# Where the first loads of float64 weights stand in a linear-attention and mixture-of-experts kernel, and where the later ones are asked for

## The chip, the cores and the metric

The kernel runs on one core of one Trainium2 chip. The metric is device microseconds (us) of one execution, the median of several runs. One profiled execution gives the rows below. PE is the matrix engine (TensorE), DVE the vector engine, ACT the scalar engine, POOL is GpSimd, and SP is the queue (SyncE) that issues the DMA transfers. Lxxx is a line of the kernel's source.

## The reference, cut to what matters

```python
def phi(x):                                   # attention feature map, 64 -> 256
    proj = einsum('bhsd,df->bhsf', x, w_phi)
    proj = proj - max(abs(proj), axis=-1)
    return concatenate([exp(proj), exp(-proj)])
q_p, k_p = phi(q), phi(k)                     # 4 batches, 8 heads, 576 rows, 64 wide
kv  = einsum('bhsf,bhsd->bhfd', k_p, v);  z = k_p.sum(axis=2)
x   = einsum('bhsf,bhfd->bhsd', q_p, kv) / (einsum('bhsf,bhf->bhs', q_p, z) + 1e-6)
x   = x as (2304, 512)
h   = x @ w_in;  x = maximum(0.01 * h, h) @ w_out     # 512 x 2048, 2048 x 512, float64
p   = probs / (probs.sum(-1) + 1e-9)                  # 2304 x 4
out = sum over 4 experts of p[:, e] * (maximum(x @ w1[e], 0) @ w2[e])
```

`w_in` and `w_out` arrive as float64, and the kernel takes them apart into float32 itself.

## The kernel before, in words

The work is four batches of attention, each followed by the first feed-forward layer on its 576 tokens, and then the four experts on all tokens. Every float32 matrix is split into a high part and a rest (`hilo`, L113), and a product is three matmuls of the parts.

**Attention.** A batch has four pairs of heads. For each pair the steps of the list STEPS run: loads of k, q and v (`kraw`, `qraw`, `v`), the projections on PE (`pq` for q, `pk` for k), the subtraction of the maximum (`mb`, `ky`), exponentials (`e`, `kp`, `kt`), the state `kvp` and `kv`, the numerator `nm` and its copy `nf`, and the division: a row of `nf` goes through DMA into `ds` (L352), is inverted on DVE (L359, L360), stored to DRAM as `dr` (L362), read back over 64 partitions as `rb` (L365), and multiplied into `xr` (L381), which is split into `xh` and `xl`.

**First feed-forward layer.** 16 tiles of 128 hidden columns for each batch: `up` (L506) makes `hp` from `xh`/`xl` and a tile of `w_in`; `hs`, `g` and `gt` are the leaky relu and its split; `down` (L538) makes `op` from four `gt` and four tiles of `w_out`. Groups of four tiles, in the order of the list ORDER.

**Float64 weights.** For the first batch `w64_dma` loads two 128 x 512 float64 tiles (1 MB) as `r64` (shown as `r` by the profile) into a pool of ten buffers. `w64_split` decodes a tile: ACT takes the high words (L460), DVE shifts and joins sign and low words (L461, L464, L467), the float32 tile `w32` is stored to DRAM (L471) for the later batches, and `hilo` splits it into `wt`. `w1_dma` and `w1_split` ask for a load and a decoding by number of tile: `w1_dma(0, F)` is `w_in`, `w1_dma(1, F)` is `w_out`, and in the first batch only even F load, two tiles at once. Later batches load `w32` back.

**Order.** The steps are sorted by hand-set times and written out in that order: `first()` loads the first weights at a set time within the attention of batch 0, `first2()` decodes the first tile, and `up(F, n)`, n = 0 and 1 for the two halves of a tile, asks for the next loads and decodings. A scheduler then simulates the engines and decides in which order each engine and the SP queue take the instructions. Those under `tc.keep_in_program_order` keep their order among themselves. Every queue and engine works in order: what waits holds up all that is behind it.

In `first()` of before, the tile loaded by `w1_dma(1, 0)` is loaded again by `up(0, 0)`, and only the second copy is read.

Of the kernel before, what the change touches and what calls it, by code (L numbers as in the profile page):

```python
# [9 lines left out]
U32 = mybir.dt.uint32  # L10
# [10 lines left out]
NF = FF1 // 128  # L21
# [58 lines left out]
def body(ctx, tc, kT, qT, vh, w_phi, w_in, w_out, probs, w1, w2, out):  # L80
    nc = tc.nc
# [336 lines left out]
    def attn(b, lo, hi):  # L418

        A = []  # L420
        for p in range(NP):
            T = TIMES[p if b == 0 else NP]
            for t, (f, h, a) in zip(T, STEPS):
                i = p if h is None else 2 * p + h
                A.append((p + t, lambda f=f, i=i, a=a: f(b, i, *a)))
        A.sort(key=lambda x: x[0])
        t0, t1 = A[0][0], A[-1][0]
        return [(lo + (hi - lo) * (t - t0) / (t1 - t0), f) for t, f in A]
# [4 lines left out]
    def w_dma(key, src):  # L433
        raw[key] = wrp.tile([128, 512], F32, tag="wr", name="wr")
        nc.sync.dma_start(out=raw[key], in_=src)

    def w_split(key, b, r=None):
        t = wp.tile([128, 2, 512], F32R, tag="w", name="wt")
        hilo(t[:, 0], t[:, 1], raw.pop(key) if r is None else r, 'w', b)
        return t  # L440

    def w64_dma(i, f):

        t = xp.tile([128, 2, 512, 2], U32, tag="x", name="r64")
        nc.sync.dma_start(
            out=t.rearrange("p a c t -> p a (c t)"),
            in_=(w_in, w_out)[i][f : f + 2].bitcast(U32).rearrange("a p c -> p a c"),
        )
        raw[i, f] = t[:, 0]
        raw[i, f + 1] = t[:, 1]  # L450

    def w64_split(i, f):

        r = raw.pop((i, f))
        lo, hi = r[:, :, 0], r[:, :, 1]
        w = wrp.tile([128, 512], F32, tag="wr", name="w32")
        wu = w.bitcast(U32)


        nc.scalar.activation(out=w, in_=hi.bitcast(F32), func=AF.Abs, scale=2.0**-112)  # L460
        nc.vector.tensor_scalar(  # L461
            out=wu, in0=wu, scalar1=3, scalar2=None, op0=ALU.logical_shift_left
        )
        nc.vector.scalar_tensor_tensor(  # L464
            out=wu, in0=hi, scalar=0x80000000, in1=wu, op0=ALU.bitwise_and, op1=ALU.bitwise_or
        )
        nc.vector.scalar_tensor_tensor(  # L467
            out=wu, in0=lo, scalar=29, in1=wu, op0=ALU.logical_shift_right, op1=ALU.bitwise_or
        )
        d = drw.tile([128, 512], F32, name=f"w32_{i}_{f}")  # L470
        nc.sync.dma_start(out=d, in_=w)  # L471
        w32[i, f] = d
        return w_split(None, 1, w)
# [4 lines left out]
    def w1_dma(i, F):  # L478
        b, f = divmod(F, NF)
        if b == 0:  # L480
            if f % 2 == 0:
                w64_dma(i, f)
        elif b < B:
            w_dma((i, F), w32[i, f])

    def w1_split(i, F):
        b, f = divmod(F, NF)
        if b < B:
            wt1[i, F] = w64_split(i, f) if b == 0 else w_split((i, F), b + 1)
# [7 lines left out]
    def moe1_up(F, n):  # L497
        x = xs[F // NF]
        wi = wt1[0, F]
        if n == 0:  # L500
            hps[F] = two("hp")
        hp = hps[F]
        for kk in range(KK):
            assert ("x", F // NF, kk) in made
            for i, (a, z) in enumerate(PASS):
                nc.tensor.matmul(  # L506
                    hp[:, n, 0:HS],
                    lhsT=wi[:, a, kk * 128 : (kk + 1) * 128],
                    rhs=x[z][:, kk, n * HS : (n + 1) * HS],
                    start=(kk == 0 and i == 0),  # L510
                    stop=(kk == KK - 1 and i == 2),
                )
        if n == 0:
            return
        hv = hp[:, :, 0:HS]
        hs = unit("hs")
        hs3 = hs.rearrange("p (a s) -> p a s", a=2)
        nc.scalar.mul(out=hs3, in_=hv, mul=0.01)
        g = unit("g")
        nc.vector.tensor_tensor(  # L520
            out=g.rearrange("p (a s) -> p a s", a=2), in0=hv, in1=hs3, op=ALU.max
        )
        gt = gp.tile([128, 2, S], F32R, tag="g", name="gt")
        hilo(gt[:, 0], gt[:, 1], g, 'g', F // NF + 1)
        gts[F] = gt
# [3 lines left out]
    def moe1_down(C, d, n):  # L529
        b, c = divmod(C, NF // GF)  # L530
        if c == 0 and d == 0 and n == 0:
            accs[b] = xp.tile([128, KK, S], F32, tag="x", name="acc")
        if n == 0:
            ops[C, d] = two("op")
        op = ops[C, d]
        for f in range(GF):
            for i, (a, z) in enumerate(PASS):
                nc.tensor.matmul(  # L538
                    op[:, n, 0:HS],
                    lhsT=wt1[1, C * GF + f][:, a, d * 128 : (d + 1) * 128],  # L540
                    rhs=gts[C * GF + f][:, z, n * HS : (n + 1) * HS],
                    start=(f == 0 and i == 0),
                    stop=(f == GF - 1 and i == 2),
                )
        if n == 0:
            return
        av = accs[b][:, d].rearrange("p (a s) -> p a s", a=2)
        if c == 0:
            nc.scalar.copy(out=av, in_=op[:, :, 0:HS])
        else:  # L550
            nc.vector.tensor_tensor(out=av, in0=op[:, :, 0:HS], in1=av, op=ALU.add)  # L551

    def moe1_group(G):


        def up(F, n):
            if n == 0:
                w1_dma(0, F + 2)
                w1_split(0, F + 1)
                w1_dma(1, F)  # L560
            elif F:
                w1_split(1, F - 1)
            moe1_up(F, n)

        def down(d, n):
            if G == B * NF // GF and d == 0 and n == 0:
                w1_split(1, G * GF - 1)
            moe1_down(G - 1, d, n)

        M = []  # L570
        for kind, i in ORDER:
            if kind == "u" and G < B * NF // GF:
                M += [lambda i=i, n=n: up(G * GF + i, n) for n in range(2)]
            elif kind == "d" and G > 0:
                M += [lambda i=i, n=n: down(i, n) for n in range(2)]
        return M
# [139 lines left out]
    def product(k, i, out, first):  # L716
        a, b = PRODUCTS[i]
        ws, xo = wo[k], xops[k // NC2][b]
        n = 0
        for kk in range(2):  # L720
            for w, z in PASS:
                kept(nc.tensor.matmul(  # L722
                    out,
                    lhsT=ws[w][:, AOPS[a], kk * 128 : (kk + 1) * 128],
                    rhs=xo[z][:, kk],
                    start=first and n == 0,
                    stop=n == 5,
                    skip_group_check=not first,
                ))
                n += 1  # L730
# [111 lines left out]
    def spread(fs, lo, hi):  # L842
        return [(lo + (hi - lo) * i / len(fs), f) for i, f in enumerate(fs)]

    def first():
        w1_dma(0, 0)
        w1_dma(1, 0)

    def first2():
        w1_split(0, 0)  # L850

    plan = attn(0, -P0, 0) + [(-P0 * (1 - FI0), first), (-P0 * (1 - FI1), first2)]
    for b in range(B):
        m = []
        for G in range(b * NF // GF, (b + 1) * NF // GF):
            m += spread(moe1_group(G), G * GF / NF, (G + 1) * GF / NF)
        if b + 1 < B:
            a = attn(b + 1, b + LO[b], b + HI[b])
        else:
            early = x2_steps(0)  # L860
            a = spread(early[:4], b + 0.1, b + 0.9)
# [27 lines left out]
    n = NB * NC2  # L889
# [3 lines left out]
    for k in range(n):  # L893
        j, c = divmod(k, NC2)
# [43 lines left out]
```

## Time and profile before

| | |
|---|---|
| median of 3 runs | 1379.69 us (1378.5 to 1380.32) |
| the profiled execution's own time | 1380.63 us |
| its span in the trace | 1378.8 us |
| mean granted clock of PE | 0.992 |
| busy: PE | 1352.1 us, 98% |
| busy: DVE | 817.8 us, 59% |
| busy: ACT | 657.9 us, 48% |
| busy: POOL | 567.8 us, 41% |
| loads of `w_in` / `w_out`, 1 MB each | 8 / 9 |

The span is the time from the first to the last instruction in the trace. The difference of 1.8 us to the execution's time lies around it. PE is idle for 26.7 us in all, most of it in the first 110 us, where attention and feed-forward layer of batch 0 and the decoding of weights share DVE and ACT.

### The profile page before, as it was taken

To read this page: it belongs to the slowest core of one execution; us is meant where nothing else is said; L and a number is where in the kernel's file an instruction comes from. 1 tells how busy PE (TensorE), PEld (TensorE's weight loads), DVE (VectorE), ACT (ScalarE), POOL (GpSimd) and SP (SyncE) were. 2 spreads that over 40 slices of the span, in tenths; PEclk is the share of its full clock that TensorE was granted. 3 is DMA by queue.
4 is the path that set the end of the run, shared out by engine and by line. 5 is a ranking of instruction groups with operands and counts; after the bars stand their busy time and mean duration, and the time that the engine had idled before them with its cause. 6 is when DMAs were issued, how large, how long until landed. Compare 5 with 4: busy or idle time off the path is not lost.

```text
span 1378.8 us, 21301 instructions
## 1 busy us (share of the span) xinstructions
PE 1352.1 (98%) x8105; PEld 1262.2 (92%) x8105; DVE 817.8 (59%) x1285; ACT 657.9 (48%) x1201; POOL 567.8 (41%) x398
## 2 busy tenths in 40 slices
PE   8979999999999999999999999999999999999998
PEld 6778999999999999998999999999999999899997
DVE  4589999678786656553555445445454444554444
ACT  5657657676576435424343443434443343433331
POOL 3211102111111000027767666767767675565651
PEclk9989999999999999999999999999999999999999
DMA  6466645333332222302212122321121232122111
GB/s 220 113 217 234 220 167 166 111 120 105 109 103 66 75 86 73 104 24 94 75 61 77 62 68 71 107 77 62 62 77 62 77 107 77 62 64 76 61 62 62
DMA packets 78518, 134.94 MB, mean 98 GB/s; under 512 B 12240, under 2 KB 22608, under 8 KB 78416
## 3 DMA queue, kind: packets, MB, share of 16 engines
q1 hardware_dynamic: 78416, 133.58, 29.8%
q8 instruction: 64, 1.05, 0.3%
q14 instruction: 38, 0.31, 0.1%
HBM read 120.30 MB, written 13.18 MB: 97 GB/s over the span
## 4 chain that ended last, share of the span: by engine, by line
PE 95%; DVE 1%; DMA 1%; issue 1%; ACT 1%; POOL 1%; SPq 0%; POOLq 0%; ACTq 0%; DVEq 0%
PE po L761 29%; PE hp L506 15%; PE op L538 14%; PE py L722 11%; PE pv L722 7%; PE px L722 7%; PE kvp L242 5%; PE nm L335 4%; PE pk L204 2%; PE pq L292 1%; PE pq L289 1%; DMA qraw<-qT 1%; POOL wul L704 0%; DMA r<-w 0%; DMA ds<-nf 0%
## 5 line engine op out<-in xcount | busy, mean ns | idle before, releaser
L761 PE MATMUL po<-wd,gh 128*128 128x512 f32 x1152 | 387.7, 391 | 0.9 <-POOL wd L714 0.9
L777 DVE SCALAR_TENSOR_TENSOR ob<-po,pe,ob 128x512 f32<-128x512 f32 x270 | 201.6, 749 | 216.6 <-PE po L761 216.6
L761 PEld LDWEIGHTS po<-wd,gh 128*128 128x128 f32 x1152 | 216.6, 188 | 42.3 <-POOL wd L714 1.3
L761 PE MATMUL po<-wd,gl 128*128 128x512 f32 x576 | 226.2, 393 | 0.0
L538 PE MATMUL op<-gt,wt 128*128 128x288 f32 x1536 | 219.9, 297 | 1.5 <-DVE gt L118 0.8
L296 POOL PARTITION_ALL_REDUCE mb<-pc x32 | 72.3, 2266 | 355.7 <-ACT pc L294 294.7
L506 PE MATMUL hp<-xh,wt 128*128 128x288 f32 x1024 | 216.2, 298 | 0.0
L538 PEld LDWEIGHTS op<-gt,wt 128*128 128x128 f32 x1536 | 207.9, 188 | 2.9 <-DVE gt L118 1.0
L506 PEld LDWEIGHTS hp<-xh,wt 128*128 128x128 f32 x1024 | 167.5, 188 | 1.0 <-ACT wt L117 0.3
L506 PE MATMUL hp<-xl,wt 128*128 128x288 f32 x512 | 151.8, 297 | 0.0
L714 POOL TENSOR_TENSOR wd<-r,wd 128x1024 fp32r<-128x1024 f32 x48 | 114.9, 2394 | 89.4 <-ACT wd L710 89.4
L722 PE MATMUL py<-xo,wuh 128*128 128x384 f32 x576 | 148.3, 339 | 0.7 <-DVE pz L827 0.7
L682 POOL TENSOR_TENSOR rs<-r 128x256 f32<-128x256 f32 x96 | 71.1, 741 | 188.8 <-DMA r<-w 188.8
L704 POOL TENSOR_TENSOR wul<-rs,wuh 128x1024 fp32r<-128x1024 f32 x48 | 115.5, 2406 | 65.9 <-ACT wuh L699 65.9
L704 POOL TENSOR_TENSOR wul<-r,wuh 128x768 fp32r<-128x768 f32 x48 | 88.8, 1851 | 85.7 <-ACT wuh L699 85.7
L761 PEld LDWEIGHTS po<-wd,gl 128*128 128x128 f32 x576 | 108.2, 188 | 15.2
L722 PEld LDWEIGHTS py<-xo,wuh 128*128 128x128 f32 x576 | 104.9, 188 | 4.6 <-DVE pz L827 1.0
L722 PE MATMUL px<-xo,wuh 128*128 128x384 f32 x384 | 98.9, 338 | 0.7 <-DVE acc L551 0.7
L722 PE MATMUL pv<-xo,wuh 128*128 128x384 f32 x384 | 99.1, 339 | 0.0
L722 PE MATMUL py<-xo,wul 128*128 128x384 f32 x288 | 97.3, 338 | 0.0
L506 PEld LDWEIGHTS hp<-xl,wt 128*128 128x128 f32 x512 | 96.3, 188 | 0.4
L807 ACT COPY py<-px 128x384 f32<-128x384 f32 x48 | 22.2, 463 | 143.4 <-PE px L722 137.3
(114 smaller groups left out, 2349.9 us busy)
## 6 DMA issues: line engine op xcount, KB each, us to landing
r<-w SPq DMA_DIRECT2D x192, 256.0 KB, 2.8
wr<-w SPq DMA_DIRECT2D x96, 256.0 KB, 2.7
qraw<-qT SPq DMA_DIRECT2D x32, 288.0 KB, 3.7
r<-w_out SPq DMA_DIRECT2D x9, 1024.0 KB, 9.0
r<-w_in SPq DMA_DIRECT2D x8, 1024.0 KB, 6.2
w<-w SPq DMA_DIRECT2D x32, 256.0 KB, 2.8
v<-vh SPq DMA_DIRECT2D x16, 480.0 KB, 4.0
kraw<-kT SPq DMA_DIRECT2D x16, 288.0 KB, 4.0
```

The source lines that it names most:

```text
L204: nc.tensor.matmul(o, lhsT=x[:, cs], rhs=w, start=(i == 0), stop=(i == len(P) - 1))
L242: nc.tensor.matmul(kvp[:, a * 128 : (a + 1) * 128], lhsT=lhs, rhs=v[:, c, h * D : h * D + 128], start=(c == 0), stop=(c == 4),)
L296: nc.gpsimd.partition_all_reduce(mb, pc, 128, bass_isa.ReduceOp.absmax)
L335: nc.tensor.matmul(o, lhsT=a[:, 2 * (h % 2) + j], rhs=x[:, j * HS : (j + 1) * HS], start=(j == 0 and i == 0), stop=(j == 1 and i == len(P) ...
L506: nc.tensor.matmul(hp[:, n, 0:HS], lhsT=wi[:, a, kk * 128 : (kk + 1) * 128], rhs=x[z][:, kk, n * HS : (n + 1) * HS], start=(kk == 0 and i ...
L538: nc.tensor.matmul(op[:, n, 0:HS], lhsT=wt1[1, C * GF + f][:, a, d * 128 : (d + 1) * 128], rhs=gts[C * GF + f][:, z, n * HS : (n + 1) * HS ...
L682: kept(nc.gpsimd.tensor_tensor(out=o, in0=x, in1=y, op=op))
L704: kept(nc.gpsimd.tensor_tensor(out=lo[:, at], in0=(r[:, 1:4], s)[i], in1=hi[:, at].bitcast(F32), op=ALU.subtract))
L714: kept(nc.gpsimd.tensor_tensor(out=d[:, 1], in0=r2, in1=d[:, 0].bitcast(F32), op=ALU.subtract))
L722: kept(nc.tensor.matmul(out, lhsT=ws[w][:, AOPS[a], kk * 128 : (kk + 1) * 128], rhs=xo[z][:, kk], start=first and n == 0, stop=n == 5, ski ...
L761: kept(nc.tensor.matmul(op, lhsT=(gh, gl)[z][:, 2 * f + t, q : q + 128], rhs=d[:, w, f], start=n == 0, stop=n == 5,))
L777: kept(nc.vector.scalar_tensor_tensor(out=o, in0=op, scalar=ps, in1=o, op0=ALU.mult, op1=ALU.add))
```

## The change

`first()` asks for the tiles 0/1 and 2/3 of `w_in`, and no longer for `w_out`. `up` leaves out the load of `w_in` for F = 0, and asks for `w_out` at n = 1 in the first batch (half a tile after `w_in`), at n = 0 later. The first batch then makes 8 loads of each. All float64 loads are kept in program order behind what was kept before them.

```diff
@@ w64_dma
-        nc.sync.dma_start(
-            out=t.rearrange("p a c t -> p a (c t)"),
-            in_=(w_in, w_out)[i][f : f + 2].bitcast(U32).rearrange("a p c -> p a c"),
+        tc.keep_in_program_order(
+            nc.sync.dma_start(
+                out=t.rearrange("p a c t -> p a (c t)"),
+                in_=(w_in, w_out)[i][f : f + 2].bitcast(U32).rearrange("a p c -> p a c"),
+            )
         )
@@ moe1_group
         def up(F, n):
             if n == 0:
-                w1_dma(0, F + 2)
+                if F:
+                    w1_dma(0, F + 2)
                 w1_split(0, F + 1)
+            if n == (F < NF):
                 w1_dma(1, F)
-            elif F:
+            if n and F:
                 w1_split(1, F - 1)
             moe1_up(F, n)
@@ body
     def first():
         w1_dma(0, 0)
-        w1_dma(1, 0)
+        w1_dma(0, 2)
```

The change adds lines, so the lines behind it are 2 to 5 higher: the loads stand at L447, the decoding at L463, L464, L467 and L470, the stores at L474, `up` at L509 and `down` at L541.

**First place: the SP queue at 9 to 25 us.** `qraw_182` is the last q load issued at 9.29 us, and `v_184` the v load of head pair 2, which shares a buffer with `v_125` of pair 0. Before:

```order
L166 DMA qraw_182<-qT 128x576
L445 DMA r64_207<-w_in 128x2x1024
L445 DMA r64_209<-w_out 128x2x1024
L161 DMA v_184<-vh 128x5x192
L166 DMA qraw_226<-qT 128x576
L471 DMA w32_0_0_476<-w32_471 128x512
```

And now:

```order
L166 DMA qraw_182<-qT 128x576
L161 DMA v_184<-vh 128x5x192
L447 DMA r64_207<-w_in 128x2x1024
L447 DMA r64_209<-w_in 128x2x1024
L166 DMA qraw_226<-qT 128x576
L474 DMA w32_0_0_476<-w32_471 128x512
```

Both float64 loads moved behind `v_184`, and the second is now of `w_in`.

**Second place: ACT, and PE, at 25 to 36 us.** `w32_471` and the next `w32` are the decoding of the first two tiles of `w_in`, `pc` is the eviction of a `pq`, `kp` and `kt` are exponentials of k. ACT before:

```order
L460 ACTIVATE w32_471<-r64_207 128x512
L460 ACTIVATE w32_621<-r64_207 128x512
L227 ACTIVATE kt_170<-pk_214 128x256 x2
L342 COPY nf_221<-nm_222 128x288
L342 COPY nf_228<-nm_229 128x288
L294 COPY pc_244<-pq_241 128x576
L117 CAST wt_478<-w32_471 128x512
L342 COPY nf_228<-nm_233 128x288
L294 COPY pc_251<-pq_248 128x576
L342 COPY nf_221<-nm_237 128x288
```

And now:

```order
L227 ACTIVATE kt_170<-pk_214 128x256 x2
L342 COPY nf_221<-nm_222 128x288
L342 COPY nf_228<-nm_229 128x288
L294 COPY pc_244<-pq_241 128x576
L463 ACTIVATE w32_471<-r64_207 128x512
L463 ACTIVATE w32_619<-r64_207 128x512
L227 ACTIVATE kp_297<-pk_299 128x1024 x2
L342 COPY nf_228<-nm_233 128x288
L294 COPY pc_251<-pq_248 128x576
L342 COPY nf_221<-nm_237 128x288
L463 ACTIVATE w32_673<-r64_209 128x512
```

The decoding and the two `kp` now stand ahead of `pc_251`, and a third tile is decoded behind it. On PE the difference of the two orders reads, from the last `nm` of head pair 0:

```order
 L335 MATMUL nm_237<-e_189,kv_202 128x288 x2
 L289 MATMUL pq_324<-qraw_182,wraw_89 128x288 x2
+L289 MATMUL pq_363<-qraw_226,wraw_89 128x288 x2
 L242 MATMUL kvp_262<-v_125,kp_169 128x128 x4
 L242 MATMUL kvp_262<-v_125,kt_170 128x128
```

`pq_363`, which stood behind `kvp_262` and `pk_309`, moved ahead of the 20 matmuls of `kvp_262`. It reads `qraw_226`, and writes the PSUM buffer that `pc_251` empties.

**Third place: the SP queue and DVE at 70 to 82 us.** `rb_600` is the last division of batch 0. SP before:

```order
L362 DMA dr_598<-ds_564 128x9
L445 DMA r64_619<-w_in 128x2x1024
L445 DMA r64_631<-w_out 128x2x1024
L365 DMA rb_600<-dr_598 64x576 x2
L471 DMA w32_0_2_680<-w32_675 128x512
L166 DMA qraw_654<-qT 128x576
```

And now:

```order
L362 DMA dr_598<-ds_564 128x9
L365 DMA rb_600<-dr_598 64x576 x2
L166 DMA qraw_650<-qT 128x576
L447 DMA r64_652<-w_out 128x2x1024
L474 DMA w32_1_0_730<-w32_725 128x512
L161 DMA v_759<-vh 128x5x192
```

The two 1 MB loads ahead of `rb_600` are gone, and one of `w_out` stands behind it. DVE before (`ky_650` empties the PSUM buffer that the next `pk` on PE writes):

```order
L216 TENSOR_TENSOR ky_608<-pk_603,m_606 128x512
L301 TENSOR_TENSOR mb_589<-pc_587,mb_589 128x576
L461 TENSOR_SCALAR w32_675<-w32_675 128x512
L464 SCALAR_TENSOR_TENSOR w32_675<-r64_619,w32_675 128x512
L467 SCALAR_TENSOR_TENSOR w32_675<-r64_619,w32_675 128x512
L381 TENSOR_TENSOR xr_614<-nf_522,rb_600 64x576
L216 TENSOR_TENSOR ky_650<-pk_646,m_648 128x256
```

And now:

```order
L216 TENSOR_TENSOR ky_608<-pk_603,m_606 128x512
L381 TENSOR_TENSOR xr_614<-nf_522,rb_600 64x576
L216 TENSOR_TENSOR ky_646<-pk_642,m_644 128x256
L301 TENSOR_TENSOR mb_589<-pc_587,mb_589 128x576
L381 TENSOR_TENSOR xr_614<-nf_527,rb_600 64x576
```

The decoding of `w_in`'s third tile moved away from here, `xr_614` and the `ky` come right behind `ky_608`, and `mb_589` comes behind them.

## Rows read from the trace of the kernel before

**Rows 1.** The page's chain that ended last, shares of the span.

```profile
PE 95%; DVE 1%; DMA 1%; issue 1%; ACT 1%; POOL 1%; SPq 0%; POOLq 0%; ACTq 0%; DVEq 0%
```

**Rows 2.** Waits of PE, 0 to 260 us: total, times, longest.

```profile
PE pk L204 <- issue: 5.3, 1, 5.3
...
PE nm L335 <- ACT nf L342: 1.7, 1, 1.7
```

**Rows 3.** Timeline of SP, 10 to 25 us: start, duration, instruction.

```profile
10.80 0.38 SPq L445 DMA_DIRECT2D r<-w_in  x1
11.22 0.47 SPq L445 DMA_DIRECT2D r<-w_out  x1
23.54 0.37 SPq L161 DMA_DIRECT2D v<-vh  x1
24.01 0.47 SPq L166 DMA_DIRECT2D qraw<-qT  x1
```

**Rows 4.** DMA issues from 70.5 to 74 us: count, KB each, median us to landing.

```profile
r<-w_in SPq DMA_DIRECT2D x1, 1024.0 KB, 6.1
r<-w_out SPq DMA_DIRECT2D x1, 1024.0 KB, 8.7
rb<-dr SPq DMA_DIRECT2D x2, 144.0 KB, 7.6
```

**Rows 5.** The same, issued from 94.6 to 95 us.

```profile
r<-w_out SPq DMA_DIRECT2D x1, 1024.0 KB, 9.1
```

**Rows 6.** The same, issued from 433 to 434.5 us.

```profile
rb<-dr SPq DMA_DIRECT2D x2, 144.0 KB, 2.9
```

**Rows 7.** Timeline of ACT, 25 to 33 us.

```profile
25.37 1.22 ACT L460 ACTIVATE w<-r 128x512 f32<-128x512 f32 x2
...
30.25 0.66 ACT L294 COPY pc<-pq 128x576 f32<-128x576 f32 x1
30.78 0.43 ACT L342 COPY nf<-nm 128x288 f32<-128x288 f32 x1
...
31.75 1.97 ACT L227 ACTIVATE kp<-pk 128x1024 f32<-128x1024 f32 x2
```

**Rows 8.** Timeline of PE, 30 to 32 us.

```profile
30.36 1.14 PE L289 MATMUL pq<-qraw,wraw 128*128 128x288 f32 x4
31.33 0.94 PE L242 MATMUL kvp<-v,kp 128*128 128x128 f32 x7
```

**Rows 9.** Timeline of PE from 38 us and from 60 us, one `nm` step each.

```profile
38.92 4.04 PE L335 MATMUL nm<-e,kv 128*128 128x288 f32 x16
...
60.46 5.84 PE L335 MATMUL nm<-e,kv 128*128 128x288 f32 x16 [2.04 <-ACT kv L252]
```

**Rows 10.** Stretches: PE, PEld, DVE, ACT, POOL busy us (instructions); PEclk; DMA share; GB/s.

```profile
61.00:64.00 3.00, 3.00 (x8) 2.07 (x7) 0.00 (x0) 0.48 (x2) 0.00 (x0) 0.51 0.84 224
85.00:88.00 3.00, 3.00 (x16) 3.00 (x16) 3.00 (x6) 0.23 (x1) 0.00 (x0) 0.53 0.00 0
104.00:108.00 4.00, 2.34 (x11) 1.48 (x10) 4.00 (x10) 4.00 (x9) 0.00 (x0) 1.00 1.02 415
103.00:138.00 35.00, 33.15 (x228) 31.09 (x229) 34.35 (x62) 26.96 (x55) 5.34 (x2) 1.00 0.66 235
```

**Rows 11.** Timeline of DVE, 72 to 83 us; in brackets idle before, and its releaser.

```profile
77.77 0.43 DVE L461 TENSOR_SCALAR w<-w 128x512 uint32<-128x512 uint32 x1 [3.11 <-ACT w L460]
...
80.47 0.75 DVE L381 TENSOR_TENSOR xr<-nf,rb 64x576 f32<-64x576 f32 x1 [0.82 <-DMA rb<-dr]
81.14 0.41 DVE L216 TENSOR_TENSOR ky<-pk,m 128x256 f32<-128x256 f32 x1
```

**Rows 12.** Timeline of SP, 70.5 to 74 us.

```profile
72.73 1.10 SPq L365 DMA_DIRECT2D rb<-dr  x2
```

**Rows 13.** Timeline of PE, 73 to 90 us.

```profile
74.26 2.05 PE L242 MATMUL kvp<-v,kp 128*128 128x128 f32 x8
81.66 2.05 PE L204 MATMUL pk<-wraw,kraw 128*128 128x256 f32 x4 [5.35 <-issue]
```

## Prediction

> **What bounds the kernel now.** I first read the chain that ended last: PE makes 95% of it [rows 1], so the time is PE's work plus its waits. The matmuls after the change are the same in number, and their order differs only between 12 and 260 us; behind that, whatever PE has won or lost is carried to the end one for one. So the next view is PE's waits in that stretch [rows 2]. One of them is large: 5.3 us ahead of a `pk`, for which the view names no releaser ("issue"); the second of interest is 1.7 us ahead of an `nm`. The timeline of DVE gives the releaser of the first [rows 11]: the `ky` that empties the PSUM buffer of that `pk` starts at 81.14, behind an `xr` that waited for the DMA into `rb` and ended its idle time at 80.47; PE goes on at 81.66 [rows 13]. Ahead of it DVE sat idle 3.11 us for ACT's decoding of a `w_in` tile. And `rb` was late because of what the SP queue had ahead of it: its two issues at 72.73 [rows 12] took 7.6 us to land beside 2 MB of float64 weights [rows 4], against 2.9 us for the same transfer later on [rows 6]. The reader should see one chain: 2 MB issued just ahead of 288 KB, `rb` late, `xr` late, `ky` late, PE idle.
>
> The clock adds to each longer wait. After the 2.04 us wait at 60.46 an `nm` step took 5.84 us, against 4.04 for the same 16 matmuls at 38.92 [rows 9], and the granted clock was 0.51, that is 1.2 GHz in the stretch from 61 us [rows 10]. At 74.26 the clock was low again (eight `kvp` in 2.05 us [rows 13], seven in 0.94 at 31.33 [rows 8]), and after the 5.35 us wait it was still 0.53 from 85 us to 88. After the 1.66 us wait it was 1.00, in the stretch from 104 us [rows 10].
>
> **The change, step by step.**
>
> *The dead load.* Between 11 and 20 us one transfer of 1 MB changes place and source. It is worth nothing by itself: none of PE's longer waits between 13 and 49 us names a transfer, and those in rows 2 lie far behind.
>
> *The first loads, 11 to 34 us.* Now `v_184` is ahead of them. Its buffer comes free at 23.54 [rows 3]; SP waits there, and behind it stand both float64 loads and `qraw_226`. With the 0.37 to 0.47 us that an issue takes in these rows, the loads go out at about 24.0 and 24.45 (before: 10.80 and 11.22), and `qraw_226` at 24.95 instead of 24.01. The first load lands 6.1 us later [rows 4], at 30.1. ACT then has, in its new order, two decodings (1.22), two `kp` (1.97), an `nf` (0.43) and `pc_251` (0.66) [rows 7]: with some 0.3 us of overlap between them `pc_251` ends at 34.0. `pq_363`, which PE now reaches at 31.33 (the place of the first `kvp` of before [rows 8]), needs that `pc_251` and `qraw_226`. The latter is the last of 2,816 KB in the queue, which took 9.1 us from its issue where the same amount stood in line [rows 5]: 34.05. Both releasers agree, and PE waits some 2.6 us: **+2.6**. Below, were the load to take only a fixed 2.2 us (2.9 for 288 KB, less 0.7 at 415 GB/s [rows 6, 10]) and 2.5 us at that rate, 4.7 in all, the wait would be 1.2. Above, with the two loads sharing evenly, the mean of 6.1 and 8.7 [rows 4], it would be 3.9. I take the row of a load that was first in a pair, as this one is.
>
> The Trainium skill ("DMA: Bandwidth & Descriptors", section "Anatomy of one DMA — SWDGE (gpsimd) path") gives a fit of 2.0 us plus the bytes over 436 KB per us, for transfers issued from GpSimd. By it the load would take an estimated 4.4 us and the wait would be 0.9 us; the row, of SP's queue, says 6.1 and decides.
>
> *What the wait drags along.* 2.6 us is longer than the 2.04 after which the clock fell, so the 20 `kvp` behind it run at the low level at first: **+1.8**, the difference in rows 9; 0 if it behaves as after 1.66 us. One more tile is decoded behind (three DVE operations of 0.4 to 0.75 us like those of rows 11), ahead of the division of pair 0; DVE has room for most of it: **+0.5**, between 0 and 1.8 (all three on the path). Up to 70 us everything is then 4.9 us late, and the steps below count from there.
>
> *The stall at 76 to 88 us.* `rb` has no weights ahead of it now. Counted in the times of before, it lands at 72.73 + 2.9 = 75.65; `xr` (0.75) and `ky` (0.41) follow at once, since the decoding that DVE waited for has moved away: PE goes on at 76.9 instead of 81.66: **-4.8**. The wait left is about 0.6 us, and the low clock, which lay over the 6.2 us from 81.66 to 87.83 and so cost 3.1, costs about 0.5: **-2.6**. What covers the `w_out` load that is now behind `rb`: issued some 1.5 us later than the first load was, alone, it lands 6.1 us on, near 80.8, and its decoding is not on PE's path until `down` at 116.
>
> *103 to 116 us.* The wait of 1.7 us [rows 2] ends on `nf` in a crowd on ACT and DVE (4.00 of 4 us busy each at 104 to 108 [rows 10]) that four loads issued together made; with loads issued one by one it dissolves: **-1.7**. In its place stands what DVE, 34.35 of 35 us busy from 103 us on [rows 10], now does later: `mb_589` is behind `xr_614` and `ky_646`, and the fourth `w_in` tile is decoded after two of `w_out`. Walking the new orders with the durations of before, I find PE waiting 1.0, 0.5 and 0.85 us: **+2.35**, from 0 (DVE keeps its lead) to 4 (nothing of the crowd goes).
>
> *116 to 260 us.* Each 1 MB load now waits its turn on SP behind stores and behind `kraw` and `v`, and each is half a tile from its neighbour. It takes 6.1 us where a pair took 6.1 and 8.7 to 9.1. DVE has no slack to give (the same row), so it works less ahead of PE: the walk gives 0.8 us at a `pk` and a lead that shrinks from 7 to 5 us: **+1.5**, from 0 to 6.
>
> Sum: 2.6 + 1.8 + 0.5 - 4.8 - 2.6 - 1.7 + 2.35 + 1.5 = -0.35. Against the profiled 1380.63 that is 1380.3; that execution was 0.94 above the median, so I expect **1379.3**.
>
> **The rivals.**
>
> *Faster: the first wait is short.* If the float64 load lands after 4.7 us, PE waits 1.2 us, the clock stays up as after 1.66 us, and the first part costs 1.2 + 0.5 instead of 4.9: the sum becomes -3.55, that is 1376.1, and with no loss behind 116 us, 1374.6. For it: bandwidth stands idle at 24 us, and the second load may give way to the first. Against it: no pair of loads in these rows lands its first in under 6.1 us.
>
> *Slower: the loads come too late behind 116 us.* `r64_841` (`w_out`) now stands on SP behind `kraw_823`, which waits for a buffer, and the decoding behind it is ahead of `nf` and `ky` on ACT and DVE. It decides when PE waits more than 4.6 us there (-1.85 without that term, and 2.76 for the bound): one load's latency of 6.1 us laid bare instead of 1.5 gives 1379.69 - 1.85 + 6.1 = 1383.9. For it: DVE is full, and a saturated engine passes lateness on. Against it: PE hardly waits between 116 and 230 us now, and a load is asked for two tiles ahead.
>
> *Slower: the loss without the rescue.* The 5.35 us have no releaser by name. If they end on something other than `rb`, such as `mb_589`, only the loss of 4.9 us stays, with part of the low clock regained: 1379.69 + 4.9 - 1 = 1383.6. The Trainium skill ("DMA: Bandwidth & Descriptors", section "Rules for kernel authors") speaks for this side: issue a transfer early and wait on it late, while here a load goes from 10.80 to 24.0 us, into its consumer's path. That rows 3 show 12 us of idle queue ahead of 23.54, in which the load was hidden before, agrees with it.
>
> **How the numbers follow.** No change: 0.45. Faster: 0.33. Slower by late loads: 0.15; without the rescue: 0.07. The kernel's runs lie within 0.13%, so 0.2%, 2.76 us, is about what a measurement can tell: faster is below 1376.9, slower above 1382.45. The likeliest case reaches from 1376.5 to 1382.5; some of its chance falls outside. That makes 0.37 faster, 0.42 same, 0.21 slower. For 8 in 10 the range goes from the faster case's 1374 to 1384.
>
> **What would show it.** Right: SP issues `v_184` at 23.5 and the loads behind it; PE waits 2 to 3 us ahead of a `pq` at about 31, with the clock at half behind it; `rb` at 78 lands in about 3 us; the 5.35 us wait is gone, and PE runs at full clock from about 83. Wrong: a wait at 31 under 1.5 us (faster), a wait of 3 us or more between 85 and 110, or several behind 116 us on `nf`, `ky` or `gt` (slower). The forecast falls altogether if `rb` still takes over 5 us.

## The result, and the profile after

The changed kernel takes 1387.07 us (median of 4 runs), the kernel before 1380.01 us (4 runs): ratio 1.0053, 95% interval 1.004 to 1.0065. It is slower by about 7 us, outside the range that was forecast. The profiled execution took 1387.26 us, with a span of 1384.9 us.

PE's waits from 0 to 260 us, after (answers to [rows 2]; total us, times, longest):

```profile
PE pq L289 <- DMA qraw<-qT: 4.4, 4, 2.8
...
PE nm L335 <- ACT kv L252: 3.5, 2, 2.0
PE pq L292 <- DVE qr L276: 3.1, 2, 2.2
PE op L541 <- DVE g L523: 1.9, 1, 1.9
PE nm L335 <- DVE ky L216: 1.4, 1, 1.4
PE kvp L242 <- issue: 1.2, 1, 1.2
...
PE op L541 <- ACT gt L117: 0.5, 1, 0.5
```

The 5.3 us "issue" wait ahead of a `pk` is gone but for 0.3. New are 2.8 us ahead of a `pq`, 1.9 ahead of an `op`, 1.4 ahead of an `nm` and 1.2 ahead of a `kvp`. The early places, first the SP queue and PE at 20 to 34 us (answers to [rows 3, 8]):

```profile
21.95 0.38 SPq L161 DMA_DIRECT2D v<-vh  x1
22.37 1.04 SPq L447 DMA_DIRECT2D r<-w_in  x2
23.51 0.41 SPq L166 DMA_DIRECT2D qraw<-qT  x1
```

```profile
28.77 1.13 PE L289 MATMUL pq<-qraw,wraw 128*128 128x288 f32 x4
32.66 1.21 PE L289 MATMUL pq<-qraw,wraw 128*128 128x288 f32 x4 [2.76 <-DMA qraw<-qT]
33.70 1.05 PE L242 MATMUL kvp<-v,kp 128*128 128x128 f32 x8
```

```profile
32.59 0.65 ACT L294 COPY pc<-pq 128x576 f32<-128x576 f32 x1
```

The loads stand behind `v`, `qraw` behind the loads, and PE waits 2.76 us for it. The `pc` (`pc_251`) ends at 33.24, when PE is already at work again, so PE did not wait for it. The eight `kvp` behind that wait take 1.05 us, so the clock did not fall. Then the stall of before: the DMA issues from 75 to 76.8 us, and PE behind them (answers to [rows 4, 13]):

```profile
rb<-dr SPq DMA_DIRECT2D x2, 144.0 KB, 3.6
```

```profile
77.49 1.91 PE L242 MATMUL kvp<-v,kp 128*128 128x128 f32 x8
79.67 1.10 PE L204 MATMUL pk<-wraw,kraw 128*128 128x256 f32 x4 [0.27 <-issue]
```

`rb` lands in 3.6 us instead of 7.6, the wait shrinks to 0.27 us, and the `pk` runs at full clock. That rescue was real. To see where it went, I compare when PE starts its 381st, 1101st and 1501st matmul and its last: before 89.10, 193.95, 247.56 and 1374.59 us; after 84.38, 191.76, 252.04 and 1380.61 us. So PE is 4.7 us ahead at 89 us, 2.2 ahead at 194, 4.5 late at 248 and 6.0 late at the end.

The largest loss is that between 191 and 206 us. Four timelines of the change tell it: SP, ACT, DVE, PE.

```profile
184.18 0.32 SPq L474 DMA_DIRECT2D w<-w  x1
184.55 0.43 SPq L447 DMA_DIRECT2D r<-w_out  x1
```

In the kernel before, the same load, the last but one of `w_out`, went out 15 us earlier:

```profile
169.55 0.43 SPq L445 DMA_DIRECT2D r<-w_out  x1
```

```profile
190.99 0.67 ACT L463 ACTIVATE w<-r 128x512 f32<-128x512 f32 x1 [2.95 <-DMA r<-w_out]
192.68 0.64 ACT L521 ACTIVATE hs<-hp 128x576 f32<-128x576 f32 x1
```

```profile
183.47 0.69 DVE L470 SCALAR_TENSOR_TENSOR w<-r,w 128x512 uint32<-128x512 uint32 x1
191.69 0.43 DVE L464 TENSOR_SCALAR w<-w 128x512 uint32<-128x512 uint32 x1 [1.79 <-ACT w L463]
192.15 0.69 DVE L467 SCALAR_TENSOR_TENSOR w<-r,w 128x512 uint32<-128x512 uint32 x1
192.88 0.76 DVE L276 TENSOR_TENSOR qr<-qraw,qr 64x576 fp32r<-64x576 f32 x1
193.66 0.76 DVE L523 TENSOR_TENSOR g<-hp,hs 128x576 f32<-128x576 f32 x1
```

```profile
194.48 1.69 PE L541 MATMUL op<-gt,wt 128*128 128x288 f32 x9 [1.89 <-DVE g L523]
196.66 6.97 PE L541 MATMUL op<-gt,wt 128*128 128x288 f32 x30 [0.49 <-ACT gt L117]
```

Read from the top: SP stands 3.1 us at a store, which goes out as DVE ends the decoding of a tile (183.47 + 0.69), and the `w_out` load goes right behind it. ACT waits 2.95 us for the load, DVE 1.79 us for ACT. The `g` that PE needs stands behind the decoding in DVE's order, and the `hs` that `g` reads stands behind it in ACT's order and ends at 193.32. So the late load reaches PE mainly through ACT; DVE's order adds 0.3 us at most. PE's two waits are 2.4 us; the 30 `op` behind them take 6.97 us because the clock has fallen, as the stretches show (last figures: PEclk, DMA share, GB/s):

```profile
192.00:196.00 4.00, 2.11 (x14) 1.69 (x12) 3.53 (x6) 2.35 (x5) 0.00 (x0) 0.94 0.75 265
196.00:200.00 4.00, 3.51 (x13) 3.05 (x13) 3.81 (x8) 3.27 (x7) 0.00 (x0) 0.50 0.43 131
```

Who waited for the float64 loads issued from 100 to 235 us, after (total us, times); in the kernel before the same answer is 1.5 us in 2. And what the stores on SP waited for in that stretch:

```profile
  ACT w L463: 12.3, 6
```

```profile
SPq L474 <- DVE w L470: 48.5, 19, 4.4
```

In the kernel before, the stores wait too (35.8 us in 18 for the same operation).

A last 1.5 us is lost at 635 to 640 us, at the first products of the experts, where PE waits for POOL's first weights:

```profile
636.79 0.45 PE L727 MATMUL pv<-xo,wul 128*128 128x384 f32 x1 [0.83 <-POOL wul L709]
639.12 1.12 PE L766 MATMUL po<-wd,gh 128*128 128x512 f32 x2 [0.89 <-POOL wd L719]
```

### The profile page after: what moved, and what is told of

Same layout as the page of the kernel before. It is cut to its first block, busy times and chain, and to the rows that moved or that the text cites. A ratio compares the mean times of both kernels' runs of the same rounds, so it can differ in the third digit from the quotient of the medians.

```text
span 1384.9 us, 21295 instructions
## 1 busy us (share of the span) xinstructions
PE 1353.4 (98%) x8105; PEld 1261.7 (91%) x8105; DVE 821.0 (59%) x1285; ACT 657.8 (47%) x1201; POOL 567.0 (41%) x398
## 4 chain that ended last, share of the span: by engine, by line
PE 84%; DVE 7%; DMA 6%; issue 1%; ACT 1%; SPq 1%; POOL 0%; DVEq 0%; ACTq 0%; POOLq 0%
PE po L766 29%; PE op L541 12%; PE hp L509 11%; PE py L727 11%; PE px L727 7%; PE pv L727 7%; PE kvp L242 3%; PE nm L335 2%; DMA r<-w_in 1%; DMA qraw<-qT 1%; DMA r<-w_out 1%; PE pk L204 1%; DVE w L467 1%; DVE w L470 1%; DMA w<-w 1%
## 5 line engine op out<-in xcount | busy, mean ns | idle before, releaser
L541 PE MATMUL op<-gt,wt 128*128 128x288 f32 x1536 | 222.8, 299 | 4.9 <-DVE g L523 2.6
L541 PEld LDWEIGHTS op<-gt,wt 128*128 128x128 f32 x1536 | 210.5, 190 | 7.5 <-DVE g L523 3.1
L509 PE MATMUL hp<-xh,wt 128*128 128x288 f32 x1024 | 216.2, 298 | 0.3 <-ACT pc L294 0.3
L509 PEld LDWEIGHTS hp<-xh,wt 128*128 128x128 f32 x1024 | 167.0, 188 | 1.2 <-ACT pc L294 0.5
L509 PE MATMUL hp<-xl,wt 128*128 128x288 f32 x512 | 151.3, 296 | 0.2 <-DVE xl L118 0.2
L766 PEld LDWEIGHTS po<-wd,gl 128*128 128x128 f32 x576 | 108.2, 188 | 15.4
L727 PEld LDWEIGHTS py<-xo,wuh 128*128 128x128 f32 x576 | 104.9, 188 | 4.7 <-DVE pz L832 1.0
L509 PEld LDWEIGHTS hp<-xl,wt 128*128 128x128 f32 x512 | 96.1, 188 | 0.9 <-DVE xl L118 0.4
```

Of the source, the lines that this page charges most:

```text
L509: nc.tensor.matmul(hp[:, n, 0:HS], lhsT=wi[:, a, kk * 128 : (kk + 1) * 128], rhs=x[z][:, kk, n * HS : (n + 1) * HS], start=(kk == 0 and i ...
L541: nc.tensor.matmul(op[:, n, 0:HS], lhsT=wt1[1, C * GF + f][:, a, d * 128 : (d + 1) * 128], rhs=gts[C * GF + f][:, z, n * HS : (n + 1) * HS ...
L727: kept(nc.tensor.matmul(out, lhsT=ws[w][:, AOPS[a], kk * 128 : (kk + 1) * 128], rhs=xo[z][:, kk], start=first and n == 0, stop=n == 5, ski ...
L766: kept(nc.tensor.matmul(op, lhsT=(gh, gl)[z][:, 2 * f + t, q : q + 128], rhs=d[:, w, f], start=n == 0, stop=n == 5,))
```

## The experiments

Two theories stood first: P, that the pin on the loads is the cause, and H, that it is the half tile by which `w_out` is asked for later. Behind them came L (loads that land late are waited for) and V (DVE, nearly full, sets the pace by itself). The table has all kernels but p2 and p3, which come below: median, ratio to the kernel before run beside it with its interval, what ACT waited in all for the float64 loads of 100 to 235 us, and how far PE is behind (+) or ahead (-) of the trace of before at the 381st, 1101st and 1501st matmul.

| kernel | us | ratio (95%) | ACT's wait | 381 | 1101 | 1501 |
|---|---|---|---|---|---|---|
| the change | 1387.07 | 1.0053 (1.004-1.0065) | 12.3 | -4.7 | -2.2 | +4.5 |
| e1_no_pin | 1381.87 | 1.0016 (1.0007-1.0026) | 3.1 | -3.9 | +1.3 | +1.5 |
| e2_same_half | 1391.50 | 1.0089 (1.0074-1.0104) | 11.7 | +4.0 | +4.5 | +13.3 |
| e3_dead_gone | 1379.33 | 1.0000 (0.9991-1.001) | 1.5 | -2.6 | -2.5 | -2.1 |
| e4_pin_only | 1388.17 | 1.0063 (1.0048-1.0078) | 10.8 | -2.1 | +2.4 | +7.4 |
| e5_first_only | 1379.90 | 1.0007 (0.9998-1.0016) | 1.6 | -3.8 | -4.0 | -0.8 |
| m1_store_pool | 1389.89 | 1.0079 (1.0064-1.0094) | 0.7 | +0.6 | +6.4 | +9.9 |
| m3_first_free | 1386.13 | 1.0044 (1.003-1.0059) | 15.4 | -8.0 | -2.3 | +4.8 |
| m6_one_pin | 1383.07 | 1.0026 (1.0013-1.0039) | 2.1 | -7.1 | -2.5 | +3.3 |
| n1_lead | 1389.29 | 1.0077 (1.0061-1.0093) | 2.4 | -4.4 | +9.1 | +9.0 |
| m8_late_free | 1382.39 | 1.0028 (1.0017-1.0039) | 9.6 | -3.2 | -1.4 | +1.6 |
| v1_after_nosign | 1376.13 | 0.9975 (0.9965-0.9985) | 2.6 | -2.0 | -3.0 | -3.6 |
| v2_before_nosign | 1380.19 | 1.0008 (0.9998-1.0017) | none | -1.1 | -0.9 | +0.5 |
| m10_ends_free | 1379.56 | 1.0000 (0.999-1.001) | 9.8 | -6.2 | -2.8 | -0.3 |
| m12_rb_first | 1376.39 | 0.9974 (0.9964-0.9984) | 0.4 | -8.7 | -5.3 | -4.5 |

Every one of these profiles has PE 0.7 to 1.9 us ahead of the profile of before at the 81st matmul already (24.75 us there), whichever edit it has, and e3's median is that of before. The trace of before therefore seems to have an early delay of its own, which was not tried; differences between kernels of the table are free of it.

ACT's wait in all does not rank the kernels: m10 has 9.8 us at the time of before, m1 0.7 us and is slower than the change. It tells where loads were late, not what that cost.

**e1_no_pin.**

```diff
-        tc.keep_in_program_order(nc.sync.dma_start(...))
+        nc.sync.dma_start(...)
```

> The change without the pin on the float64 loads: the first two loads go out ahead of v_184 again, and the later ones where the scheduler puts them, mostly in pairs. Theory P (the pin is the cause: it holds a load behind a store that waits for DVE, as the w_out load at 184.55 us that landed at 190.89 and was waited for by ACT's decoding, then DVE, then PE's op at 194.5): the 2.8 us wait ahead of a pq at 31 us is gone, and so is the 6.4 us lost from 191 to 206; the time falls by 5 to 9 us from 1387.1 to 1378 to 1382. Rival H (the half tile by which the w_out load is asked for later is the cause): the loss from 191 to 206 stays, and only the 31 us wait goes: 1384 to 1387.

It gave 1381.87 us: most of the loss goes with the pin. Next to nothing is lost at 191 us (0.3 us between the 1101st and the 1160th matmul), but 4 us between 151 and 172, around this wait of PE:

```profile
159.84 4.21 PE L538 MATMUL op<-gt,wt 128*128 128x288 f32 x20 [1.97 <-DVE wt L118]
```

**e2_same_half.**

```diff
-            if n == (F < NF):
+            if n == 0:
                 w1_dma(1, F)
```

> The change with w_out asked for at n = 0, together with w_in, in the first batch too; the pin stays. Theory P: w_out is issued right behind w_in, but both still behind the stores; the loss around 191 us shrinks by little, time 1385 to 1388, and the wait at 31 us stays at 2.8. Rival H: the w_out load is issued some 3 us earlier than at 184.55, the op wait at 194 goes, and the time is 1379 to 1382.

Slower still, 1391.5 us, beyond P's range too: as a cause of the time, H fails. With the pin, the half tile saves 4.4 us. But H had a point on the place: between the 1101st and the 1160th matmul this kernel loses 1.2 us and the change 6.4. What is lost here is lost elsewhere: PE waits 4.0 us, to 34.4 us, where the change waits 2.76, and from the 1160th to the 1501st matmul it loses 7.6 us.

**e3_dead_gone.**

```diff
     def first():
         w1_dma(0, 0)
-        w1_dma(1, 0)
```

> The kernel before without its unused first load of w_out, and nothing else changed. The profile of the change shows PE 1.6 us ahead at 20 us, with its pq wait at 12 us 1.7 us shorter. Theory D (the unused 1 MB, beside w_in, slows the early q load and the low clock follows): the pq starts near 12 us or sooner at full clock, 1378 to 1379, about -1.6. Rival N (w_in alone does the same, or the difference is one between executions): within 0.7 us of before, 1379.5 to 1380.5.

No difference in the median (N): the unused load was hidden.

**e4_pin_only.** The kernel before, with the load in `tc.keep_in_program_order`.

> The kernel before with the pin on the float64 loads alone (unused load kept, w_out asked for with w_in). Theory P: v_184 goes ahead of the loads, PE waits 2 to 3 us at 31 us, the 5.35 us wait at 81 us goes, and the loads behind 116 us are held behind stores: 1383 to 1388. Rival H: the rescue at 81 us stays and nothing is lost later: 1375 to 1380.

1388.17 us: the pin alone costs as much as the whole change, so for the time P is right. The places differ. This kernel loses 4.5 us from the 381st to the 1101st matmul, 0.7 from there to the 1160th, and 4.3 from there to the 1501st. Among these kernels the large loss at 191 to 206 us shows only in the change and m3, which have both the pin and the half tile.

**e5_first_only.**

```diff
     def first():
         w1_dma(0, 0)
-        w1_dma(1, 0)
+        w1_dma(0, 2)
@@ up
-                w1_dma(0, F + 2)
+                if F:
+                    w1_dma(0, F + 2)
```

> The first edit alone: w_in's tiles 0/1 and 2/3 loaded first, no unused load, no pin, and w_out asked for with w_in. Compared with the change without the pin (1381.87, w_out half a tile later, 3 us lost at 155 to 172) it tells what the half tile does without the pin. Theory P (loads in pairs, issued early, are never waited for): no loss behind 116 us, 1377 to 1380. Rival F (decoding a third tile early costs more than it saves): 1381 or more.

1379.9 us, as before. Without the pin the half tile seems to cost 1 to 2 us (e1 against e5), but the two intervals overlap, so that this is not shown; with the pin it saves.

**m1_store_pool.**

```diff
-        nc.sync.dma_start(out=d, in_=w)
+        nc.gpsimd.dma_start(out=d, in_=w)
         w32[i, f] = d
```

> The change with the stores of the decoded tiles issued from POOL's queue instead of SP's, so that the pinned loads no longer stand behind stores that wait for DVE; nothing else is moved by hand, the scheduler orders anew. Theory S (the stores are what a pinned load waits for on SP): ACT's wait for float64 loads between 100 and 235 us falls from 12.3 us to under 4, the loss at 191 to 206 goes, the wait at 31 us stays: 1379 to 1383. Rival O (other transfers ahead of them, kraw and v with their buffer waits, or the order of asking itself, hold them): ACT's wait stays at 8 us or more and the time at 1385 to 1388.

ACT's wait falls from 12.3 to 0.7 us, and PE loses nothing between matmuls 1101 and 1160: the stores were what the loads waited for on SP. But the time is 1389.89 us. PE stands 6.4 us late at the 1101st matmul already, from losses at 31, 52, 118 and 165 us in an order that the scheduler made anew. That the loads wait for the stores is borne out, as by the 3.1 us above; that the time falls when they do not is not. Neither theory's range holds the time.

**m3_first_free.** Pinned unless `(i, f)` is `(0, 0)` or `(0, 2)`; i is 0 for `w_in` and 1 for `w_out`, f the first tile of the pair.

> The change with the first two loads left out of the pin (they go out ahead of v_184, as before the change), the others pinned. It measures the early price of the pin. Theory P: no wait at 31 us, so 3 to 4.5 us less by 60 us, and the loss from 191 to 206 stays: 1382.5 to 1384.5. Rival: the early loss is absorbed at the stall of 76 us, so the time stays 1386 to 1388.

The wait at 31 us goes and PE is 8.0 us ahead at 89 us, 3.3 more than the change; at the 1101st matmul both are 2.2 to 2.3 ahead. Only 0.9 us reaches the median. The rival had the time right and the place wrong: the lead outlives the stall of 76 us and is given back between 89 and 167 us.

**m6_one_pin.** Pinned only if `(i, f)` is `(1, 0)`, with the half tile.

> The change with only w_out's first load pinned (asked for at n = 1, so behind the division's rb), all other loads free. The early wait does not exist, rb has no weights ahead of it (gain at 76 to 88 us), and later loads are not held by the pin. Theory P with the half tile harmless: 1373 to 1378, the fastest so far. Rival H2 (the half tile makes w_out late without the pin too, as in the change without the pin, which lost 3 us at 155 to 172): 1378 to 1382.

1383.07 us, just beyond H2. From 7.1 ahead, 4.6 are given back by the 1101st matmul, and 5.9 more behind it.

**n1_lead.**

```diff
-                if F:
-                    w1_dma(0, F + 2)
+                if F + 4 < NF:
+                    w1_dma(0, F + 4)
+                elif F + 2 >= NF:
+                    w1_dma(0, F + 2)
                 w1_split(0, F + 1)
-            if n == (F < NF):
-                w1_dma(1, F)
+                if F == 0:
+                    w1_dma(1, 0)
+            if n == (F < NF):
+                if F >= NF:
+                    w1_dma(1, F)
+                elif F + 2 < NF:
+                    w1_dma(1, F + 2)
```

> The change, pin and half tile kept, with every float64 load of the first batch after the first two asked for one pair of tiles earlier (w_in four tiles ahead of the tile in hand instead of two, w_out two instead of none). Theory L (what costs behind 116 us is that the decoding waits for the load): ACT's wait for float64 loads from 100 to 235 us falls from 12.3 us to under 4, DVE's idle time in that stretch falls by some 5 us, and the 6.4 us lost at 191 to 206 go: 1380 to 1383, the wait at 31 us still there. Rival O (DVE's order, not the loads, is the loss): ACT's wait falls and the time stays at 1385 to 1389.

ACT's wait falls to 2.4 us and the loss at 191 us goes, as in m1, but 13.6 us are lost ahead of it, from the 381st to the 1101st matmul, nearly all before the 601st. More decoding is now crowded in there: by the 601st, DVE has begun 16 tiles, in the change 11. That this is the cause was not tried. ACT's wait fell as L said; the time did not, and comes nearest to rival O.

**p2_after_pool and p3_dead_gone_pool.** The rest part of a decoded tile on POOL.

```diff
+        if r is not None:
+            nc.scalar.copy(out=t[:, 0], in_=r)
+            nc.gpsimd.tensor_tensor(
+                out=t[:, 1], in0=r, in1=t[:, 0].bitcast(F32), op=ALU.subtract
+            )
+            return t
```

> The change with the rest part of each freshly decoded weight tile (one 128x512 subtraction of about 0.68 us on DVE, 32 in the first batch, 22 us in all) made on POOL, which is almost idle before 260 us. Theory V (from 85 to 240 us DVE is the engine that sets the pace, so its idle time is paid in full and PE's lead is worth nothing): 6 us or more faster than the change, 1378 to 1381 or below. Rival L (only the late loads matter): the loss at 191 to 206 stays, 1385 to 1388.

> The kernel before without its unused load, and with the rest parts of the decoded tiles on POOL as above. Theory V: PE's waits behind 90 us go as far as they come from DVE, 1374 to 1378, faster than before. Rival: PE was not held by DVE there (it waits for little between 110 and 230 us in the kernel before), so 1378.5 to 1381, or slower if POOL's part comes late for PE.

Neither tells V from L: 1459.5 us (ratio 1.0578, 1.0561 to 1.0596) and 1459.83 us (1.059, 1.0574 to 1.0605). POOL's subtraction took 1434 ns, and it stands in POOL's order among reductions that wait for ACT. Of PE's waits up to 330 us in p3:

```profile
PE op L544 <- POOL wt L441: 21.5, 3, 8.9
```

**m8_late_free.** Pinned unless `(i, f)` is `(0, 14)`, `(1, 12)` or `(1, 14)`.

> The change with only its last three float64 loads left out of the pin (w_in 14/15, w_out 12/13 and 14/15). SP's queue is the same up to 170 us; then w_in 14/15 and w_out 12/13 go out together, ahead of two stores and a v, instead of at 180.88 and 184.55. Theory L: nothing differs up to 190 us, the op waits at 192 to 197 and the low clock behind them go, 5 to 7 us less: 1380 to 1382. Rival V: DVE is late there by its own work; the wait only changes its name, and the time stays at 1385 to 1388.

1382.39 us, just beyond L's range and 4.7 less than the change (3.5 by the ratios to the kernel before run beside each). The first two of the three loads go out at 171.74 and 172.41 us instead of 180.88 and 184.55. PE passes the place with this wait instead of 1.9 and 0.5 us, and without the low clock (granted 1.00 from 196 to 200 us):

```profile
196.03 2.13 PE L540 MATMUL op<-gt,wt 128*128 128x288 f32 x14 [1.06 <-DVE gt L118]
```

Between the 1101st and the 1160th matmul it loses 2.2 us instead of 6.4. Late loads and the clock behind them thus make 4.2 us of the loss; the other 2.2 remain with the loads early, and their cause was not tried.

**v1_after_nosign and v2_before_nosign.** Both without the operation that joins the sign.

```diff
-        nc.vector.scalar_tensor_tensor(
-            out=wu, in0=hi, scalar=0x80000000, in1=wu, op0=ALU.bitwise_and, op1=ALU.bitwise_or
-        )
```

> The change without the DVE operation that joins the sign bit (the weights lose their sign, so this leaves out part of the computation): 32 operations of 0.69 us, 22 us of DVE's work up to 225 us. Theory V (DVE sets the pace from 85 to 240 us): 5 us or more less than the change, also outside 191 to 206. Theory L alone (loads that come late): the loss at 191 to 206 stays within 2 us and the time is 1384 to 1388.

> The kernel before, with the same operation left out. Theory V: the time falls by more than 2 us, 1372 to 1377. Rival: before had DVE just ahead of PE everywhere behind 110 us, so the 22 us are slack: 1377.5 to 1380.

The change gains 10.9 us (1376.13), the kernel before nothing (1380.19). The scheduler orders anew in both. DVE's work is slack in the kernel before, so V is wrong for this stretch as such. In the change it is not slack: the time fell as V expected, and L alone, which expected 1384 or more, is wrong there. DVE's own work and late loads are not told apart by it: the stores on SP go earlier too, the loads that went out at 180.88 and 184.55 us in the change go out at 177.33 and 178.34 us, and ACT's wait falls to 2.6 us.

**m10_ends_free.** Pinned unless `(i, f)` is among the five of m3 and m8.

> The change with the first two and the last three float64 loads left out of the pin. It has no wait at 31 us and should have none at 192 to 206. Theory L: as the change with only the last loads free, less at most 1 us (the early gain was gone by 160 us in the change with only the first loads free): 1378 to 1381. If the early 3 to 5 us were kept: 1374 to 1377.

1379.56 us, the time of before, within L's range.

**m12_rb_first.** As e5, with `w_out`'s first load alone pinned and half a tile later.

```diff
-            if n == (F < NF):
+            if n == (F == 0):
                 w1_dma(1, F)
@@ w64_dma
+        if (i, f) == (1, 0):
+            tc.keep_in_program_order(ins)
```

> The first edit, with only w_out's first load asked for half a tile later and pinned (so behind the division's rb), every later load free and in pairs. It keeps the gain at 76 to 88 us and should lose nothing to late loads. Theory L: ACT's wait for float64 loads behind 100 us at 2 us or less, no loss behind 116 us, 1374 to 1378, faster than before. Rival V (an early lead of PE dissolves into DVE's work by 240 us anyhow, as with the two ends free): 1378 to 1381.

1376.39 us against 1379.91 beside it: the only version with the reference's computation that beats both. Who waited for its loads:

```profile
  ACT w L462: 0.4, 1
```

## Why the prediction was wrong

- **The first loads, +2.6 with +0.5 and +1.8 behind it: the wait right, the clock wrong.** The wait was 2.76 us. Of the two releasers that should agree, only the transfer of `qraw` held PE, 9.0 us behind its issue where 9.1 were forecast; the load that `pc_251` was priced by played no part. The clock did not fall behind it, and at 60 to 64 us it was granted in full (1.00), where it had fallen before. Up to matmul 301 the change is 1.08 us behind the trace of before, from 1.59 ahead: 2.7 us in place of 4.9.
- **The stall, -4.8 and -2.6: right in kind, a little large.** From 1.08 behind, PE is 4.72 ahead at the 381st matmul: -5.8 instead of -7.4. The transfer of 3.6 us and the 0.27 us wait show the mechanism.
- **103 to 116 us, -1.7 and +2.35: right in kind, too small.** Forecast +0.65, measured +2.4, from 4.72 ahead at 89 us to 2.3 ahead at 112. The 1.7 us wait on `nf` did dissolve. In its place PE has waits of 0.9, 1.4 and 1.2 us that end at 92.5, 100.7 and 104.9 us, where 1.0, 0.5 and 0.85 were forecast.
- **116 to 260 us, +1.5, from 0 to 6: the step that failed.** It measured 6.8 us (2.3 ahead to 4.5 behind), nearly all between 191 and 206: above the term's own upper bound. I costed each load by its own 6.1 us and DVE by its mean load, and took the lead of DVE to absorb the rest. What the runs showed: the pin puts a load behind stores that wait for DVE (m1), 15 us later than before, so it lands late; ACT waits for it, and `hs` on ACT and `g` on DVE, which PE needs, stand behind that in order. With the loads free, 2.2 of the 6.4 us are left there (m8). The rival of loads that come too late had 0.15. It named `kraw` and its buffer as what holds a load; at 181 and 184 us it was a store.
- **The wait behind the wait.** I priced that rival at one laid-bare latency, 6.1 us, without the clock: 1383.9 against the measured 1387.07. The 30 `op` at 196 us took 6.97 us, where 30 of them took 4.15 us in the kernel before: 2.8 us more.
- **"Whatever PE has won or lost is carried to the end one for one"** was off by 1.5 us: at 635 to 640 us the changed arrival of PE met POOL's first weights. m3_first_free loses 1.4 us there too, the other kernels of the table 0.4 at most; what decides it was not tried.
- **The unused load, 0: right** (e3).
- **The rule on early issue.** The rule of the Trainium skill ("DMA: Bandwidth & Descriptors", section "Rules for kernel authors") to issue a transfer early and wait on it late pointed the right way, but at the wrong load: at 31 us its cost hardly reached the end (m3 against the change, 0.9 us), behind 180 us it did (m8). Asking earlier for all loads but the first two did not help either (n1, 1389.29 us).

That the change is slower is shown to be the pin (e4, e1, m10); that its early gain could be had without it is shown by m12. Shown for the change alone is the chain at 191 to 206 us; where the pin is paid for depends on the order that the scheduler makes, and not every place was followed to its cause. The 2.4 us given back at 89 to 112 us were not pursued: m3, m6, m10 and m12, which start further ahead, give back 2.7 to 4.4 there.

## What to carry to other kernels

To get one small transfer out from behind two large ones, move those two; a pin on all transfers of a kind also put every later one behind stores that wait for their producers. A load's price is not its latency but what stands in order behind the engine that waits for it, and a lead of PE need not reach the end: of the 3.3 us by which m3 led the change at 89 us, 0.9 did. Moving one thing made the scheduler order the rest anew (m1, n1), so that a mended wait did not mend the time. Sum a change over the whole stretch in which the order moves: the end with the saved wait was forecast to within 1.6 us, and the end with no wait in the trace of before decided.

## What was not expected of the hardware

After PE's 2.76 us wait at 31 us the clock stayed high (eight `kvp` in 1.05 us), while it fell after waits of 2.04 us in the kernel before [rows 9], and after 1.89 and 0.49 us close together at 192 to 197 us (granted 0.50). The plainest pair is one and the same `nm` step behind one and the same wait: in the kernel before it took 5.84 us, in the change it ran at full clock:

```profile
63.22 4.15 PE L335 MATMUL nm<-e,kv 128*128 128x288 f32 x16 [2.04 <-ACT kv L252]
```

The length of a single wait did not decide it in these traces, and what did was not tried.
